# V's weight behind K's on one queue, a skip term seeded by VectorE, a scan over every sixteenth token, and a new step list, in a gated mix of a state-space layer and linear attention

## The chip, the cores and the metric

One core of one Trainium2 chip. The metric is device time in microseconds, median of the runs; lower is better. ACT is ScalarE, DVE is VectorE, PE is TensorE, POOL is GpSimd, SP is SyncE, which here only issues DMAs.

## The reference, cut to what matters

```python
x = A_x                                       # [1, 2048, 512], bf16
g = sigmoid((x * gate_w).sum(-1))             # one gate per token
# a: diagonal complex state space, 512 states
dt = exp(log_dt); Lam_bar = exp(dt * Lam)
Bu = x @ (((Lam_bar - 1) / Lam)[:, None] * Bmat).T
for t in range(2048):
    h = Lam_bar * h + Bu[t]                   # hseq[t] = h
a = 2 * (hseq @ Cmat.T).real + x * Dskip
# b: linear attention, 32 heads of 16, features softmax(+p) and softmax(-p)
q, k, v = split(x @ wqkv)
phi_q, phi_k = feat(q @ w_phi), feat(k @ w_phi)     # 32 features a head
b = ((phi_q @ (phi_k.T @ v)) / (phi_q @ phi_k.sum(0) + 1e-6)) @ wo
out = g * a + (1 - g) * b
```

## The kernel before

The 2048 tokens are 16 tiles of 128, ordered by residue: with NR = 8, tile pair r holds the tokens t with t mod 8 = r, 256 of each residue (NC = 256). `x_load` brings each tile transposed into `xT` by a DMA on SP's queue.

The whole kernel is one hand-written order. Each step is a generator (`st_k`, `st_g`, ...) that yields after each of its parts. The text `ORDER` names which step's next part is issued, the PSUM banks that it takes (`k3@6`), and the engine that empties PSUM where that isn't ACT (`:D` for DVE; `:A` puts an output DMA on ACT's queue). Instructions of PE, DVE, ACT and SP stand on each engine in that order; nothing is reordered. An instruction whose data or bank isn't ready stops its engine.

The steps, in about the order of their places in the list:

- W, f, w fold `w_phi` into K's and Q's weight. V, U, P, P2, P3, P4 and M make the decay constants, M on POOL; i makes Sin and Cos tables `T2s`, `T2c` on ACT over NC columns; D builds the diagonal blocks `dg`.
- k and v multiply `xT` with K's and V's weight; ACT copies the results out of PSUM into `Xq` and `vx`. v computes both 256-column halves of a tile in one step and takes two banks. V's weight `Wv` comes by one DMA on SP's queue between two groups of x tiles; K's comes on ACT's queue.
- x, n, e, s turn K into features, for five groups of tiles: maximum and minimum trees on DVE (x, n), Exp on ACT (e), sum trees on DVE, then Ln and Exp of the sums on ACT (s). a accumulates features times V. X, N, E, S do the same for Q.
- g (residue r, state block j) is B times x plus, for odd r, two earlier residues through `dg`: a recurrence unrolled over eight tokens. ACT copies it into `uv`, for r = 7 into `va`. z runs the scan over every eighth token on DVE, 256 columns: rotate by the tables, scan with r^8, rotate back, write into `H7`. h then gets the other residues' states from `H7`.
- q, c (scale C on ACT, add on DVE), y (states times C, then x times the diagonal `Dd` on PE for the skip term, into one PSUM bank), o (features times KV, Ln and Exp on ACT for the division, product on DVE, transpose), t (times `wo` onto the same bank, scaled by the gate into `ot`, DMA out).

Two steps set ACT's function tables. At the start, and in step L, `pin_act_set` issues a load of the set `natural_log_exp_and_others`; the Sin batch of i and P2, P3 comes between. Step L also ends the pool of the table steps and opens the pool of z. In the list of before it stands here:

```python
k6@7 R1 L e0 n1 n1 x1 n1 l13 k6:D v4@14 x1 ...
```

Of the kernel before, what the change touches and what calls it, by code (L numbers as in the profile page):

```python
# [10 lines left out]
ALU = mybir.AluOpType  # L11
# [9 lines left out]
P = 128  # L21
# [15 lines left out]
g63@0 z2 z2 v12@74 a3 nA v11 a3 xA g03 z2 z2 z2 z2 xA nA s4 J3 g63 g23@2 c5 s4 v12 g23 h51@6 g13@3 g13 g13 z2 z2 c0 z2
z2 eA g43@0 g43 eA v14@74 v14 J1 h51 s4 g33@2 g33 h52@3 g33 h12@0 g53@6 eA g53 g53 h12 h11@7 h11 h52 eA sA g73@4 g73
g73 g73 v13@26 v13 q10@0 z3 c6 z3 c5 sA z3 z3 v15@73 z3 a4 a4 a4 v15 z3 q10 q5@4 a4 Y z3 h31@0 q5 sA h30@4 z3 q9@2 h31
q13@6 h31 q9 h33@0 h61@7 Y q13 h30 sA sA c5 h62@3 z3 z3 h30 h61 sA Y Y h22@5 q4@2 h62 q4 h33 q15@6 q11@7 h22 h20@4 h20  # L40
h32@2 h32 sA sA c1 q11 h13@1 h13 h32 q14@3 h40@5 h33 c3 h53@7 h42@4 sA h42 h53 c1 c1 sA h21@2 c3 h21 q6@0 q6 q15 c6
q7@1 h63@4 h63 q8@7 h03@0 c3 q7 c6 h40 sA c7 h41@6 h41 y6@2 c7 h03 h03 h43@4 h43 y2@1 h02@5 c7 sA h23@6 h23 h01@0
h00@4 END q8 G X1 y6 y6 q14 y2 N1 X1 h00 h00 N1 y2 h02 h02 X1 N1 G h01 o0@6 y0@7 o0 o0@3 h01 o2@4 o2 X1 o2@5 o2 o2 N1
y5@6 o0 y3@0 X1 N1 y5 X2 o0 o1@4 E1 o2 y0 o2 o0 E1 E1 E1 X2 y1@5 y1 y3 y3 o1 G N2 X2 N2 X2 o0 N2 X2 o3@3 o3 o3@4 S1 o3
o3 G S1 N2 S1 t2 o3 S1 o3 t2 t2:A q12@3 q12 N2 S1 S1 o1@4 o1 o1 o1 o1 S1 S1 E2 S1 y0 y4@1 y9@3 y8@4 y8 y8 X3 E2 E2 S1
S1 S1 N3 X3 E2 t3 X3 X3 X3 S2 N3 t0 t0 t0:A S2 t3 S2 y1 t1 t1 y5 y9 y9 o4@7 o4 o4@0 o4 y4 o4 o4 o4 o5@5 o5 o5@7 o5 o5
y13@0 S2 S2 o6@5 o6 o6@7 o6 o6 y13 N3 y7@5 y7 N3 y7 y13 o5 S2 S2 N3 E3 o5 o6 o6 S2 S2 E3 E3 o7@7 o7:D y4 t4 t4:D t5
o7@7 S2 S2 E3 S3 t5 S2 S3 S3 o7 o7 o7 t6 y11@1 y11 o7 t6 o8@6 o8 o8@7 o8 o8 S3 S3 o8 y12@2 o9@6 o9 o9@7 o8 y11 y12 y12
y10@6 o9 o9 o9 o11@7 o11 o9 S3 S3 y10 y10 o11@7 t7 o11 o11 t7 t8 S3 S3 o11 o11 S3 t8 S3@7 S3:D S3@5 S3 t9 t9 t1:A
o10@4 y15@7 o10:D o10@5 o10:D t8 o10 o10 o10 y15 o12@4 o12:D o12@3 t4 o14@5 o12 o12 o12 t5 o14 t11 o14@4 o14:D o14 o14  # L50
t11 y14@3 t9:A o13@5 o13 o12@4 o12:D y14 o13@1 o13 o13 o15@4 o15:D o15@5 o15 o15 t12 t3:A t10 o13 o13@1 o15 t6:A t11
o14@4 o13:D t7 t10 t10 y15 t12 t12 o15@5 o15 y14 o14:D t13 t14 t14 t14 t13 t13 t15 t15 t15:A
"""
H_VECTOR = tuple((r, j) for r in (1, 2, 4, 5, 6) for j in range(4))
PH_PE = (14, 15)
H_SEED = tuple((r, j) for r in (0, 3,) for j in range(4))
# [14 lines left out]
def kernel(  # L71
# [27 lines left out]
    NC = S // NR  # L99
    NT2 = Pst // 64  # L100
# [7 lines left out]
    out_par = out2.rearrange("(a c r) d -> c r a d", r=NR, c=P)  # L108
# [59 lines left out]
    for k0 in (0, 2):  # L168
        nc.scalar.dma_start(out=wk_nat[:, k0:k0 + 2, :], in_=B_wqkv[k0 * P:(k0 + 2) * P, D:2 * D].rearrange("(k p) n -> p k n", p=P))
    nc.sync.dma_start(out=Wc[:], in_=B_w_phi.rearrange("(k hl) e f -> (hl e) k f", hl=8))  # L170
# [23 lines left out]
    H7 = pR.tile([P, NT2, ZP + NC], BF16, name="H7")  # L194
# [7 lines left out]
    dg = pBC.tile([P, 4, NT2, P], BF16, name="dg")  # L202
# [4 lines left out]
    par = pBC.tile([P, 22, PT], F32, name="ssm_par")  # L207
    dl = pBC.tile([P, 20, PT], F32, name="dl")
    dgB = pBC.tile([P, 10, PT, 2], F32, name="dgB")
    dgv = phT0[:, 3].rearrange("p m f -> p (m f)")[:, 0:32 * NT2].rearrange("p (k f) -> p k f", f=4)  # L210
# [10 lines left out]
    T2c = pAC.tile([P, PT, NC], BF16, name="T2c")  # L221
    T2s = pAC.tile([P, PT, NC], BF16, name="T2s")
    uv = [pAC.tile([P, 7, 2, NC], BF16, name=f"uv{j}") for j in range(PT)]
    va = [pAC.tile([P, 2, NC], BF16, name=f"va{j}") for j in range(PT)]
# [4 lines left out]
    x_res = x2.rearrange("(a c r) d -> r a c d", r=NR, c=P)  # L229
# [11 lines left out]
    nc.sync.dma_start(out=Wv, in_=B_wqkv[:, 2 * D:3 * D].rearrange("(k p) n -> p k n", p=P))  # L241
# [8 lines left out]
    iot = tabp.tile([P, NC], F32, name="iot", bufs=1)  # L250
    nc.gpsimd.iota(iot[:], pattern=[[1, NC]], base=0, channel_multiplier=0, allow_small_or_imprecise_dtypes=True)
# [15 lines left out]
    dt_, r_, om_, t0, t1, t2, den_, r2_, r4_, om8, r8_ = (par[:, 10 + k, :] for k in range(11))  # L267
# [102 lines left out]
    def st_P4():  # L370
        VS(out=om8, in0=t0, scalar1=float(NR), scalar2=None, op0=ALU.mult)
# [10 lines left out]
    def st_M():  # L382
# [24 lines left out]
        GT(out=dl[:, 9, :], in0=tb[:, 0, :], in1=den_, op=ALU.mult)  # L407
        GT(out=dl[:, 8, :], in0=tb[:, 1, :], in1=den_, op=ALU.mult)
        lo = dl[:, 0:10, :].rearrange("p (k t) j -> p k t j", t=2)
        up = dl[:, 10:20, :].rearrange("p (k t) j -> p k t j", t=2)  # L410
        GS(out=up[:, 0:4, 0], in0=lo[:, 0:4, 1], scalar1=-1.0, scalar2=None, op0=ALU.mult)
        GC(out=up[:, 0:4, 1], in_=lo[:, 0:4, 0])
        GS(out=up[:, 4, 0], in0=lo[:, 4, 0], scalar1=-1.0, scalar2=None, op0=ALU.mult)
        GC(out=up[:, 4, 1], in_=lo[:, 4, 1])
        for h in range(2):
            for ri in range(2):
                GC(out=dgB[ri * 64:(ri + 1) * 64, :, :, h], in_=dl[h * 64:(h + 1) * 64, 10 * ri:10 * ri + 10, :])
        yield

    def st_D():  # L420
        v5_ = dgv.rearrange("p (k t a) f -> p k t a f", k=4, a=2)
        b5_ = dgB[:, 0:8].rearrange("p (k a) j h -> p k a (j h)", a=2)
        for a in range(2):
            nc.vector.tensor_copy(out=v5_[:, :, :, a, :], in_=b5_[:, :, a, :].unsqueeze(3).to_broadcast([P, 4, NT2, 4]))
        VT(out=idn2[:], in0=ident[:, 0:64], in1=ident[:, 64:P], op=ALU.add)
        VT(out=dg[:].rearrange("p k t (a c f) -> p (k t a) c f", f=4, a=2),
           in0=idn2[:].rearrange("p (c f) -> p c f", f=4).unsqueeze(1).to_broadcast([P, 8 * NT2, 16, 4]),
           in1=dgv.unsqueeze(2).to_broadcast([P, 8 * NT2, 16, 4]), op=ALU.mult)
        yield
# [15 lines left out]
    def st_i(j):  # L445
        kk_ = tabp.tile([P, NC], F32, name="kk")
        VS(out=kk_[:], in0=iot[:], scalar1=om8[:, j:j + 1], scalar2=MAGIC, op0=ALU.mult, op1=ALU.add)
        yield
        psi = tabp.tile([P, NC], F32, name="psi")
# [37 lines left out]
    def st_v(ti):  # L487
        hd = D // 2
        pv = [bank([P, hd + c], F32, "pv") for c in range(2)]
        for kt in range(KT):  # L490
            for c in range(2):
                MM(out=pv[c][:], lhsT=xT[:, kt, ti * P:(ti + 1) * P], rhs=Wvg[:, kt, c * hd:(c + 1) * hd + c], start=(kt == 0), stop=(kt == KT - 1))  # L492
        yield
        for c in range(2):
            evac(vxb[ti % NVX][:, 16 * c:16 * c + 16, 0:Dh], pv[c][:, 0:hd].rearrange("p (h e) -> p h e", e=Dh))
# [369 lines left out]
```

## Time and profile before

| | |
|---|---|
| runs | 156.17, 156.59, 157.39 us; median 156.59 |
| profiled execution | span 153.7 us from first to last instruction; its time with what lies around the span is not listed |
| PE busy | 145.5 us, 95% of the span, 1238 matmuls |
| ACT busy | 136.7 us, 89% |
| DVE busy | 131.0 us, 85% |
| POOL busy | 12.9 us, 8% |
| granted TensorE clock | 0.995 |
| DMA | 17.03 MB, mean 111 GB/s |

Busy time is a share of the whole span. The kernel has stages with different limits, so busy time by stage and the chain of waits say more than these shares. In the rows of groups the time of one instruction is from its start to its end; instructions that follow each other on an engine overlap a little, so the chain's lengths, counted end to end, are shorter.

### The profile page before, as it was taken

The numbers are of one execution on the slowest core, as the hardware profiler recorded it, in microseconds if no ns is written. First come the engines' busy times: TensorE is split into PE (matmuls) and PEld (weight loads), VectorE is DVE, ScalarE is ACT, GpSimd is POOL, SyncE is SP. The second block draws the span as 40 slices with busy tenths as digits, with TensorE's granted clock in tenths as the row PEclk, the third lists the DMA queues.
The fourth block names the chain that finished last, engine by engine and source line by source line (L and its number), as shares of the span: only waits on it lengthen the run. The fifth ranks groups of instructions, "written<-read, shape, count | busy, mean of one in ns | idle before, by whom it ended". The sixth has DMA issues, their size and how long they took to land.

```text
span 153.7 us, 3412 instructions
## 1 busy us (share of the span) xinstructions
PE 145.5 (95%) x1238; PEld 99.7 (65%) x1254; DVE 131.0 (85%) x302; ACT 136.7 (89%) x322; POOL 12.9 (8%) x43
## 2 busy tenths in 40 slices
PE   7799999999999999999999999999999899999990
PEld 7656665886899858889876565554545455555550
DVE  3599999999999999999999999999999858445510
ACT  3599999999999999999999999999798897577672
POOL 8258800000000000000000000000000000000000
PEclk9999999999999999999999999999999999999998
DMA  4788995544474379960000006603139938667633
GB/s 117 162 220 121 213 171 102 102 86 92 101 102 100 80 146 205 237 133 0 2 4 2 0 0 134 125 18 68 33 82 118 215 80 194 141 118 172 211 123 102
DMA packets 48737, 17.03 MB, mean 111 GB/s; under 512 B 42064, under 2 KB 48720, under 8 KB 48720
## 3 DMA queue, kind: packets, MB, share of 16 engines
q1 hardware_dynamic: 47008, 15.36, 50.6%
q10 hardware_dynamic: 1552, 1.44, 2.9%
q8 instruction: 10, 0.16, 0.5%
q0 software_dynamic: 160, 0.01, 0.2%
q14 instruction: 7, 0.06, 0.1%
HBM read 2.64 MB, written 2.10 MB: 31 GB/s over the span
## 4 chain that ended last, share of the span: by engine, by line
ACT 48%; PE 31%; DMA 8%; DVE 6%; issue 3%; POOL 2%; ACTq 0%; POOLq 0%
PE py L734 12%; ACT EEk L140 12%; ACT uv L121 9%; PE py L782 6%; ACT vx L121 5%; PE pq L478 5%; ACT Xq L121 5%; ACT phT L603 4%; PE ph L685 3%; ACT va L121 3%; DMA phT<-EEq 3%; DMA oT<-on 3%; PE pn L753 2%; DMA vec_n<-in_A_log_dt_dram 2%; ACT EEq L140 2%
## 5 line engine op out<-in xcount | busy, mean ns | idle before, releaser
L614 PE MATMUL pgq<-xT,BT 128*128 128x256 bf16 x256 | 31.5, 272 | 0.0
L614 PEld LDWEIGHTS <-BT 128*128 128x128 bf16 x256 | 24.7, 98 | 3.5
L140 ACT ACTIVATE EEk<-EEk 128x1024 bf16<-128x1024 bf16 x20 | 21.3, 1099 | 0.0
L478 PEld LDWEIGHTS <-xT 128*128 128x128 bf16 x128 | 12.2, 97 | 11.0 <-issue 0.2
L121 ACT CAST uv<-pgq 128x512 bf16<-128x512 f32 x28 | 16.7, 638 | 0.0
L492 PE MATMUL pv<-Wv,xT 128*128 128x256 bf16 (+1 forms) x128 | 16.5, 273 | 0.1
L478 PE MATMUL pq<-Wq,xT 128*128 128x512 bf16 x60 | 15.2, 379 | 0.2
L782 PE MATMUL py<-Wo,oT 128*128 128x512 bf16 x59 | 14.7, 379 | 0.6 <-DMA oT<-on 0.3
L478 PE MATMUL pk<-Wk,xT 128*128 128x512 bf16 x60 | 14.9, 379 | 0.2
L492 PEld LDWEIGHTS <-xT 128*128 128x128 bf16 x128 | 12.5, 98 | 3.1 <-issue 0.2
L786 ACT ACTIVATE ot<-py,G 128x512 bf16<-128x512 f32 x15 | 9.8, 684 | 2.9 <-PE py L782 2.4
L140 ACT ACTIVATE EEq<-EEq 128x1024 bf16<-128x1024 bf16 x12 | 11.8, 1084 | 0.3 <-DVE EEq L535 0.3
L603 ACT ACTIVATE phT<-X,dgB 128x512 bf16<-128x512 bf16 x16 | 11.1, 751 | 0.0
L140 ACT ACTIVATE ld<-pn 128x16 f32<-128x16 f32 x32 | 6.4, 204 | 5.2 <-PE pn L753 5.0
L121 ACT CAST vx<-pv 128x256 bf16<-128x256 f32 x32 | 10.7, 435 | 0.0
L121 ACT CAST nu<-pn 128x256 bf16<-128x256 f32 x26 | 10.0, 400 | 0.0
L556 DVE TENSOR_TENSOR EEk<-EEk,rck 128x4096 bf16<-128x4096 bf16 (+1 forms) x5 | 9.3, 1860 | 0.1
L121 ACT CAST Xq<-pq 128x512 bf16<-128x512 f32 x16 | 9.0, 604 | 0.4 <-PE pn L753 0.4
L782 PEld LDWEIGHTS <-oT 128*128 128x128 bf16 x64 | 5.7, 98 | 5.7 <-DMA oT<-on 0.5
L753 PEld LDWEIGHTS <-phT 128*128 128x128 bf16 x128 | 6.4, 97 | 4.6 <-DMA phT<-EEq 1.3
L761 DVE TENSOR_TENSOR on<-nu,rd 128x512 bf16<-128x512 bf16 x16 | 6.6, 422 | 2.6 <-ACT rd L140 2.1
L519 DVE TENSOR_TENSOR smk<-smk 128x512 bf16<-128x512 bf16 (+4 forms) x18 | 8.1, 449 | 0.1
(179 smaller groups left out, 322.9 us busy)
## 6 DMA issues: line engine op xcount, KB each, us to landing
X<-HM SPq DMA_DIRECT2D x8, 256.0 KB, 4.7
out_dram<-ot SPq DMA_DIRECT2D x9, 128.0 KB, 2.2
out_dram<-ot ACTq DMA_DIRECT2D x7, 128.0 KB, 2.0
C2r<-in_B_wqkv_dram ACTq DMA_DIRECT2D x2, 256.0 KB, 3.5
Wv<-in_B_wqkv_dram SPq DMA_DIRECT2D x1, 512.0 KB, 4.0
Bn<-in_A_B_im_dram SPq DMA_DIRECT2D x1, 512.0 KB, 5.5
Bn<-in_A_B_re_dram SPq DMA_DIRECT2D x1, 512.0 KB, 5.9
Wo<-in_B_wo_dram SPq DMA_DIRECT2D x1, 512.0 KB, 5.9
```

What stands on the lines that cost most here:

```text
L121: nc.scalar.copy(out=out_ap, in_=in_ap)
L140: ins = nc.scalar.activation(**kw)
L478: MM(out=pt[:], lhsT=xT[:, kt, ti * P:(ti + 1) * P], rhs=W[:, kt, :], start=(kt == 0), stop=(kt == KT - 1))
L492: MM(out=pv[c][:], lhsT=xT[:, kt, ti * P:(ti + 1) * P], rhs=Wvg[:, kt, c * hd:(c + 1) * hd + c], start=(kt == 0), stop=(kt == KT - 1))
L519: VT(out=dst, in0=cur[:, :, :, 0:n, :], in1=cur[:, :, :, n:2 * n, :], op=op)
L556: VT(out=E5, in0=E5, in1=rc.to_broadcast([P, L, 2 * NB, Dh, 4]), op=ALU.mult)
L603: nc.scalar.mul(out=t_, in_=x_, mul=c_)
L614: MM(out=pg[:, h, :], lhsT=BT[:, kt, 2 * j + h, :], rhs=xT[:, kt, r * NC:(r + 1) * NC], start=(h == 0 and kt == 0), stop=(r % 2 == 0 and k ...
L734: MM(out=py[:], lhsT=hs(r, t, slice(a * P, (a + 1) * P)), rhs=C2B[t], start=(t == 0), stop=False)
L753: MM(out=pn[:, 4 * m:4 * m + 4, :].rearrange("p h e -> p (h e)"), lhsT=ph[:, 4 * hf + m, :], rhs=KVm[:, 4 * hf + m, :], start=(m == 0), st ...
L782: MM(out=py[:], lhsT=oT[:, g, :], rhs=Wo[:, g, :], start=False, stop=(g == HG - 1))
L786: nc.scalar.mul(out=ot[:], in_=py[:], mul=G[:, ti:ti + 1])
```

## The change

- V's weight comes in two DMAs on ACT's queue behind K's, no longer on SP's. The step v becomes two steps, u for the first 256 columns and v for the other 256 and the gate column, one bank each.
- Tokens within a residue are split by the parity of their place: the first tile of a pair holds tokens t with t mod 16 = r, the second those with t mod 16 = r + 8. The scan runs over N2 = 128 columns with r^16; g for r = 7 first forms the pair sums (`ua`, two matmuls with a new block `dg[4]`), and a new step Z gives the states of the places between.
- For the last eight tiles in order (`Y_SEED`), y starts with DVE's product x * Dskip written into the PSUM bank, and the matmuls of states and C accumulate onto it; the four `Dd` matmuls of such a tile go. A new step XN loads those x rows and Dskip on SP's queue.
- The list `ORDER` is new throughout. The F steps behind the first are gone. L stands here:

```python
s2 w0@0 x4 s2 g70 w1@3 g41 e3 e3 g62@2 x4 g11 a2 a2 g70 a2 a2 C0 s3 L g70 z0 s3 z0 ...
```

The core of the diff:

```diff
-    nc.sync.dma_start(out=Wv, in_=B_wqkv[:, 2 * D:3 * D].rearrange("(k p) n -> p k n", p=P))
+    for k0 in (0, 2):
+        nc.scalar.dma_start(out=Wv[:, k0:k0 + 2, :], in_=B_wqkv[k0 * P:(k0 + 2) * P, 2 * D:3 * D].rearrange("(k p) n -> p k n", p=P))
...
-    x_res = x2.rearrange("(a c r) d -> r a c d", r=NR, c=P)
+    x_res = x2.rearrange("(c a r) d -> r a c d", r=NR, c=P)
...
+        cmul(8, m4, m4)
...
+        GT(out=r16_, in0=r8_, in1=r8_, op=ALU.mult)
...
-    def st_v(ti):
+    def st_v(ti, c):
...
+        evac(ua[j][:], pg[:, :, 0:N2])
+        yield
+        for h in range(2):
+            MM(out=pg[:, h, N2:NC], lhsT=dg[:, 4, 2 * j + h, :], rhs=ua[j][:, h, :], start=False, stop=True, skip_group_check=True)
+        yield
         for h in range(2):
             for ri in range(2):
-                evac(va[j][h * 64:(h + 1) * 64, ri, :], pg[ri * 64:(ri + 1) * 64, h, :])
+                evac(va[j][h * 64:(h + 1) * 64, ri, :], pg[ri * 64:(ri + 1) * 64, h, N2:NC])
...
-        rb = r8_[:, j:j + 1].to_broadcast([P, NC])
+        rb = r16_[:, j:j + 1].to_broadcast([P, N2])
...
+    def st_Z(j):
+        pz = bank([P, 2, N2], F32, "pz")
+        for h in range(2):
+            MM(out=pz[:, h, :], lhsT=dg[:, 4, 2 * j + h, :], rhs=H7[:, 2 * j + h, ZP - 1:ZP - 1 + N2], start=(h == 0), stop=True, skip_group_check=True)
+        yield
+        VT(out=H7[:, 2 * j:2 * j + 2, ZP + N2:ZP + NC], in0=pz[:], in1=ua[j][:], op=ALU.add)
+        yield
...
+    def st_XN():
+        nc.sync.dma_start(out=live["Db"][:], in_=A_Dskip.unsqueeze(0).to_broadcast([P, D]))
+        yield
+        for h in range(4):
+            ti = order[8 + 2 * h]
+            for a in range(2):
+                assert order[8 + 2 * h + a] == ti + a
+            nc.sync.dma_start(out=live["xn"][:, 2 * h:2 * h + 2, :], in_=x2.rearrange("(c a r) d -> r c a d", r=NR, c=P)[ti // 2])
+            yield
...
+        if n in Y_SEED:
+            VT(out=py[:], in0=live["xn"][:, n - 8, :], in1=live["Db"][:], op=ALU.mult)
+            yield
         for t in range(NT2):
-            MM(out=py[:], lhsT=hs(r, t, slice(a * P, (a + 1) * P)), rhs=C2B[t], start=(t == 0), stop=False)
+            MM(out=py[:], lhsT=hs(r, t, slice(a * P, (a + 1) * P)), rhs=C2B[t], start=(t == 0 and n not in Y_SEED), stop=False, skip_group_check=n in Y_SEED)
             if t % 4 == 3:
                 yield
+        if n in Y_SEED:
+            return
```

More of the change, by code (lines that the diff above doesn't have):

```diff
@@ L55 @@
 PH_PE = (14, 15)
+Y_SEED = tuple(range(8, 16))
 H_SEED = tuple((r, j) for r in (0, 3,) for j in range(4))
@@ L220 @@
     BT = pAC.tile([P, KT, NT2, P], BF16, name="BT")
-    T2c = pAC.tile([P, PT, NC], BF16, name="T2c")
-    T2s = pAC.tile([P, PT, NC], BF16, name="T2s")
+    T2c = pAC.tile([P, PT, N2], BF16, name="T2c")
+    T2s = pAC.tile([P, PT, N2], BF16, name="T2s")
     uv = [pAC.tile([P, 7, 2, NC], BF16, name=f"uv{j}") for j in range(PT)]
-    va = [pAC.tile([P, 2, NC], BF16, name=f"va{j}") for j in range(PT)]
+    va = [pAC.tile([P, 2, N2], BF16, name=f"va{j}") for j in range(PT)]
+    ua = [pAC.tile([P, 2, N2], BF16, name=f"ua{j}") for j in range(PT)]
     X1 = pAC.tile([P, NT2, D], BF16, name="X1")
@@ L266 @@
     tb = par[:, 4:6, :]
-    dt_, r_, om_, t0, t1, t2, den_, r2_, r4_, om8, r8_ = (par[:, 10 + k, :] for k in range(11))
+    dt_, r_, om_, t0, t1, t2, den_, r2_, r4_, om8, r8_, r16_ = (par[:, 10 + k, :] for k in range(12))
     GT = nc.gpsimd.tensor_tensor
@@ L370, in st_P4 @@
     def st_P4():
-        VS(out=om8, in0=t0, scalar1=float(NR), scalar2=None, op0=ALU.mult)
+        VS(out=om8, in0=t0, scalar1=float(2 * NR), scalar2=None, op0=ALU.mult)
         yield
@@ L485, in st_k @@
         yield
-    def st_v(ti):
+    def st_v(ti, c):
         hd = D // 2
-        pv = [bank([P, hd + c], F32, "pv") for c in range(2)]
+        pv = bank([P, hd + c], F32, "pv")
         for kt in range(KT):
-            for c in range(2):
-                MM(out=pv[c][:], lhsT=xT[:, kt, ti * P:(ti + 1) * P], rhs=Wvg[:, kt, c * hd:(c + 1) * hd + c], start=(kt == 0), stop=(kt == KT - 1))
+            MM(out=pv[:], lhsT=xT[:, kt, ti * P:(ti + 1) * P], rhs=Wvg[:, kt, c * hd:(c + 1) * hd + c], start=(kt == 0), stop=(kt == KT - 1))
         yield
-        for c in range(2):
-            evac(vxb[ti % NVX][:, 16 * c:16 * c + 16, 0:Dh], pv[c][:, 0:hd].rearrange("p (h e) -> p h e", e=Dh))
-        nc.scalar.copy(out=gl[:, ti:ti + 1], in_=pv[1][:, hd:hd + 1])
+        evac(vxb[ti % NVX][:, 16 * c:16 * c + 16, 0:Dh], pv[:, 0:hd].rearrange("p (h e) -> p h e", e=Dh))
+        if c:
+            nc.scalar.copy(out=gl[:, ti:ti + 1], in_=pv[:, hd:hd + 1])
         yield
@@ L781, in st_t @@
         for g in range(HG):
-            MM(out=py[:], lhsT=oT[:, g, :], rhs=Wo[:, g, :], start=False, stop=(g == HG - 1))
+            MM(out=py[:], lhsT=oT[:, g, :], rhs=Wo[:, g, :], start=False, stop=(g == HG - 1), skip_group_check=n in Y_SEED)
         yield
@@ L831 @@
         next(st[tok])
-    for key in ("op", "fq", "eq", "sq"):
+    for key in ("xn", "op", "fq", "eq", "sq"):
         pools[key][0].__exit__(None, None, None)
```

142 lines of the change are left out of this document (75 added, 67 removed).

## The prediction

> **What bounds the kernel now.** I read the busy time by stage first: start and end in us, length, then PE, PEld, DVE, ACT and POOL busy with instruction counts, granted clock, DMA share and GB/s.
>
> ```profile
> 0.00:10.00 10.00, 7.81 (x73) 6.42 (x75) 5.66 (x37) 5.64 (x10) 4.92 (x17) 1.00 0.62 162
> 10.00:18.00 8.00, 7.95 (x52) 4.75 (x52) 7.93 (x29) 7.97 (x22) 7.34 (x24) 1.00 0.98 161
> 18.00:50.00 32.00, 31.87 (x310) 25.37 (x310) 31.69 (x63) 31.83 (x71) 0.66 (x3) 1.00 0.62 112
> 50.00:84.00 34.00, 33.68 (x325) 27.58 (x326) 33.67 (x69) 33.74 (x77) 0.00 (x0) 1.00 0.44 91
> 84.00:101.00 17.00, 16.70 (x105) 9.72 (x107) 16.71 (x41) 16.94 (x35) 0.00 (x0) 1.00 0.32 63
> 101.00:120.00 19.00, 18.53 (x138) 9.67 (x138) 18.64 (x36) 17.06 (x43) 0.00 (x0) 1.00 0.45 77
> 120.00:130.00 10.00, 9.91 (x80) 5.15 (x79) 7.85 (x16) 8.67 (x25) 0.00 (x0) 1.00 0.68 151
> 130.00:153.70 23.70, 19.11 (x171) 11.08 (x173) 8.86 (x20) 14.80 (x47) 0.00 (x0) 0.97 0.57 144
> ```
>
> From 18 to 101 us PE, DVE and ACT are all full; ACT has 0.49 us idle in 83. Nothing can be added to any of them there for free. After 101 us ACT and then DVE have room, and PE alone stays full.
>
> The chain that ended last says which of the three ends last (start, length, what, count). Its shares are in units of work that follow each other without a gap, so these lengths are also what one more such instruction costs a full engine.
>
> ```profile
> 19.94 0.54 ACT vx L121 x2
> 21.15 0.95 ACT EEk L140
> 29.39 0.97 ACT uv L121 x2
> 45.10 0.37 ACT va L121
> 62.68 1.83 ACT phT L603 x3
> 84.64 0.86 PE pq L478 x4
> 97.04 0.22 PE ph L685 x2
> 98.12 0.22 PE py L739 x4
> ```
>
> The chain runs on ACT from 18.9 to 84.2 us, then on PE. So ACT's list sets the first stage, PE's list the last one; from 84 to 101 us the chain names PE, but ACT is busy 16.94 of 17, so a longer ACT list lengthens that stretch as well. The hand-over that I use as a mark is the first Ln of the output steps (`ld<-pn`), which stands in ACT's timeline here, with the start of the Exp work:
>
> ```profile
> 0.79 1.07 ACTq L169 DMA_DIRECT2D C2r<-in_B_wqkv_dram  x2
> 5.39 1.07 ACT L121 COPY Xq<-ptw 128x512 bf16<-128x512 bf16 x2 [2.22 <-PE ptw L277]
> 16.93 0.64 ACT L121 CAST Xq<-pk 128x512 bf16<-128x512 f32 x1
> 17.59 1.28 ACT L132 ACT_TABLE_LOAD   x1
> 18.89 1.06 ACT L140 ACTIVATE EEk<-EEk 128x1024 bf16<-128x1024 bf16 x1
> 101.10 0.25 ACT L140 ACTIVATE ld<-pn 128x16 f32<-128x16 f32 x1
> ```
>
> **Part 1, the step list: seven more table loads on ACT.** Step L issues the pinned load of the table set that has both Exp and Ln. Before, L stands just ahead of the first e0. In the new list it stands behind all of e0 to e3, and behind s0 to s2, whose Ln and Exp alternate. Without the pinned set ahead of them the built program of the changed kernel places a load at each turn: ahead of the first EEk, then Ln, Exp, Ln, Exp, Ln, Exp of s0, s1 and s2, and L's own after them. That is 10 loads on ACT in all, where the program of before lists 3 and its trace shows these 3:
>
> ```profile
> L132 ACT ACT_TABLE_LOAD x2 | 2.6, 1283 | 1.9 <-issue 1.9
> L146 ACT ACT_TABLE_LOAD x1 | 1.3, 1283 | 0.0
> ```
>
> What a load costs is read from the timeline above: the copy ends at 16.93 + 0.64 = 17.57, the exponential behind the load at 18.89 + 1.06 = 19.95. That is 2.38 us, of which the exponential alone would take 0.95 back to back: 1.43 a load, because the load also breaks the overlap of its neighbours. 7 x 1.43 = +10.0 us. (Bounds: the bare 1.28 gives 9.0, less the 0.5 that ACT idles; the upper end is a rival below.) Behind each load wait the copies that empty PSUM for k, v and g tiles; PE waits for their banks, DVE for PE's tiles.
>
> The Trainium skill's page "ScalarE: Activation LUTs", section "What ACT_TABLE_LOAD costs", puts a switch at 1283 ns plus about 1380 ns of drain, 2.66 us. By that the seven would be 18.6 us, 8.6 more than my term. The trace agrees on the 1283 and shows no such drain: 0.02 us lie between 17.57 and 17.59.
>
> **The rest of ACT's list up to the first `ld`.** Four `ua` copies of 128x256 at 0.54/2 = +1.1. The scan over every sixteenth token halves the columns of `va` and of the Sin tables: two `vx` of 256 columns take 0.54 and two `uv` of 512 take 0.97, so 128 columns are 0.11. `va` goes from 16 x 0.37 to 14 x 0.26 = -2.3 (two move to DVE). Eight Sin at -0.11 = -0.9. One Wk, one Xq, one uv copy (0.49 each) and one phT scaling (1.83/3) go to DVE: -2.1. Two Wk copies of 0.49 stand behind the first `ld` now: -1.0. ACT's list to the first `ld`: 10.0 + 1.1 - 2.3 - 0.9 - 2.1 - 1.0 = **+4.8 us**.
>
> **PE behind that mark.** Behind its first `pn` PE has 8 more matmuls of 512 columns (0.86/4 each), 6 more of 256 (0.22/2), and 28 fewer of 128 (0.22/4): 1.7 + 0.7 - 1.5 = **+0.8 us**. The 32 `Dd` matmuls dropped for eight tiles are 1.8 us of PE in the whole, and 16 new ones of 128 columns (on `ua`, and Z) give 0.9 back; the list moves other work behind the mark.
>
> **DVE.** The skip term is eight 128x512 products into PSUM, which no row shows. The nearest are a 128x512 add out of PSUM and one within SBUF:
>
> ```profile
> L689 DVE TENSOR_TENSOR HM<-ph,uv 128x512 bf16<-128x512 f32 x8 | 5.3, 682 | 0.0
> L519 DVE TENSOR_TENSOR mxk<-mxk 128x512 bf16<-128x512 bf16 x4 | 1.7, 418 | 0.0
> L654 DVE TENSOR_TENSOR_SCAN w<-ssm_par,ut 128x256 bf16<-128x256 f32 x8 | 5.1, 675 | 0.0
> ```
>
> I take the PSUM row, 0.6 to 0.68, 5 us in all; by the SBUF row 3.3. Five of them stand behind 120 us, where DVE idles 2.15 of 10 and then 14.8 of 23.7 us: nothing. Three stand ahead of the second group's rho product, where DVE is full: 0 to 2.0, and they delay that group's phT transposes and the matmuls on them. I take **+0.6**, one of three, since the idle time just behind takes the others. What is saved in the scan steps (at most half of 5.1 us of scans; four new adds from PSUM at 0.68 take 2.7 back), in the tables, and the larger D are worth nothing either way while ACT's list ends last; were ACT not late, each DVE us would count, as DVE idles 0.6 us in these 66.
>
> **Start and queues.**
>
> ```profile
> 6.58 0.58 SPq L241 DMA_DIRECT2D Wv<-in_B_wqkv_dram  x1
> 61.75 2.23 SPq L304 DMA_DIRECT2D X<-HM  x3
> SPq L775 <- DVE mxq L519: 5.8, 1, 5.8
> L829 PE MATMUL spin<-fillw 128*128 128x128 bf16 x36 | 3.9, 292 | 1.1 <-DVE fillw L159 1.1
> ```
>
> V's weight behind K's adds two issues, 1.07 us, ahead of ACT's first table load; ACT then idles 2.22 us for PE anyway, so 0. If its bytes delay K's, whose landing PE awaits, up to +1. SP loses 0.58 us of issue ahead of x tiles 4 to 7, so their k steps can start up to 0.6 earlier, and V's halves fill PE there. Eight fill matmuls go (8 x 0.055). ACT idles 4.4 us of its first 10; I take **-0.4** (bounds -1.0 and +1.0).
> SP gets five more issues, Db and four of xn, at 2.23/3 = 0.74 each, among the oT transposes. SP waits 5.8 us for DVE there at one place alone, so nothing; without that cover the oT transposes behind them are up to 3.7 us later, and the last projections with them. POOL's longer M stands on an engine with 0.66 us of work from 18 to 50: nothing, and late it would hold D on DVE. x tiles and output rows keep 1 KB rows at another stride: nothing.
>
> **The sum.** 4.8 + 0.8 + 0.6 - 0.4 = +5.8 us on the profiled span of 153.7, 159.5. The median of the runs shown is 156.59, 2.9 us over the span (start and end around it, taken as unchanged): 162.4 us.
>
> **Rivals.**
> (a) As summed, the loads paid in full: 162.4; its own range 159.5 to 165.5, from loads at 9.0 less idle time, seeds at 0 and the early start, up to all three seeds, a late K weight and ACT's lateness passed on to DVE and back. For it: ACT's 0.49 us idle in 83. Chance 0.62.
> (b) Not slower: the loads go unpaid. Place: ACT from 18 to 50 us. A load waits for no data, so it can run while the Ln or Exp behind it waits for DVE's sum; in the new list ACT has 5.2 us less of other work in the stage, so it may wait there. Price: the 10.0 falls away, -5.2 + 0.8 + 0.6 - 0.4 = -4.2, 152.4 us. It decides once ACT would wait some 6 us beside the loads before 84 us. Against it: PE and DVE have no more than 0.7 us to give, so they would make ACT wait only if they themselves are slower. Chance 0.10.
> (c) Half of it: loads hidden in part, PE's list ends last, with 0.9 fewer matmul us, -0.4 at the start and +0.6 for the seeds: 155.9, no difference. Chance 0.10.
> (d) The tail gives way too: all three seeds and SP's five issues on the path, 162.4 + 1.4 + 3.7 = 167.5. For it: DMA 0.68 busy from 120 to 130 us, PE with 0.1 idle. Against: SP's waits. Chance 0.14.
> (e) A load lets ACT run empty first, for as long as a whole 1.06 us exponential: 7 x 1.06 = 7.4 more, 169.8. Against: 0.02 us in this trace. Chance 0.04. (That is the skill's drain, named above, at a price from rows.)
>
> **How the numbers follow.** Likeliest: 162.4. The range 156.0 to 168.0 takes in (a), (d) and the upper half of (c) and leaves out (b), (e) and the other half, 0.19. A difference under 1%, 1.6 us, can hardly be told from none here: faster 0.10 from (b), same 0.10 from (c), slower 0.80 from (a), (d), (e).
>
> **What would show it.** Right: ten ACT_TABLE_LOADs, eight between 15 and 55 us, each 1.28 long and with no gap before it; ACT still full from 18 us; the first `ld` at 105 to 107 us instead of 101.1; PE with 4 to 6 us more of idle between 18 and 60, ended by ACT's copies; from the first `ld` to the end 53 to 55 us (52.6 before). Seeds near 0.65. Wrong: the first `ld` at 100 us or earlier although the loads are there (then ACT's list did not bind), fewer than ten loads, or a lengthening that lies behind the first `ld`.

## The result, and the profile after

| | before | after |
|---|---|---|
| runs | 156.17 to 157.39 us, median 156.5 (4) | 165.32 to 165.65 us, median 165.46 (4) |
| profiled execution | span 153.7 us | span 163.3 us, time 165.32 us |
| start of the first Exp of the features | 18.89 us | 18.79 us |
| first `ld` (the prediction's mark) | 101.10 us | 107.65 us |
| from the mark to the end | 52.6 us | 55.65 us |

The changed kernel is slower: ratio 1.0574, 95% interval 1.054 to 1.0608. The forecast was 162.4 us with a range of 156.0 to 168.0. Between the first Exp and the mark 6.65 us are lost, behind the mark 3.05. Two of the kernels further down had one slow run each, at a lower granted clock, which is left out of their figures.

The busy time by stage, after, with the same columns as in the prediction:

```profile
18.00:50.00 32.00, 28.63 (x235) 21.51 (x236) 25.67 (x50) 31.72 (x61) 5.16 (x16) 0.95 0.62 115
50.00:84.00 34.00, 30.50 (x314) 25.35 (x313) 31.05 (x75) 33.61 (x73) 0.00 (x0) 1.00 0.35 71
84.00:101.00 17.00, 16.89 (x149) 12.21 (x150) 16.86 (x40) 16.88 (x39) 0.00 (x0) 1.00 0.07 14
101.00:120.00 19.00, 18.82 (x136) 10.47 (x137) 18.71 (x41) 17.79 (x44) 0.00 (x0) 1.00 0.71 131
120.00:130.00 10.00, 9.64 (x71) 4.88 (x71) 9.29 (x19) 8.44 (x23) 0.00 (x0) 1.00 0.85 167
```

From 18 to 84 us ACT is as full as before (65.33 of 66 us). PE has fallen from 65.55 to 59.13 us and DVE from 65.36 to 56.73: both now wait for ACT, which has no more to give. What fills ACT are the loads, here in its timeline (start, length, operation):

```profile
17.50 1.28 ACT L144 ACT_TABLE_LOAD   x1
18.79 1.06 ACT L144 ACTIVATE EEk<-EEk 128x1024 bf16<-128x1024 bf16 x1
...
26.93 1.28 ACT L144 ACT_TABLE_LOAD   x1
29.02 1.28 ACT L144 ACT_TABLE_LOAD   x1
33.53 1.28 ACT L144 ACT_TABLE_LOAD   x1
36.11 1.28 ACT L144 ACT_TABLE_LOAD   x1
...
47.77 1.28 ACT L144 ACT_TABLE_LOAD   x1
49.76 1.28 ACT L144 ACT_TABLE_LOAD   x1
54.27 1.28 ACT L136 ACT_TABLE_LOAD   x1
```

The groups after have them as one row, seven loads with 0.1 us of idle ahead of all of them:

```profile
L144 ACT ACT_TABLE_LOAD x7 | 9.0, 1283 | 0.1
```

With L's own and two at the start there are ten. They come in pairs: Ln, then back to Exp, for the sums of s0, s1 and s2. The waits of PE and DVE up to the mark name the same place (engine, line and what it waited for, us in total, times, longest):

```profile
DVE EEk L563 <- ACT rck L144: 6.2, 3, 2.9
PE pv L499 <- ACT vx L125: 2.4, 1, 2.4
PE pgq L621 <- ACT uv L125: 1.7, 1, 1.7
PE pgq L621 <- ACT va L125: 1.1, 1, 1.1
```

`rck` is the Exp behind the second load of a pair. DVE waits three times, 2.9 us at the longest, before it can scale the features; PE waits for the copies that stand behind the loads.

### The profile page after: what moved, and what is told of

Its sections match the earlier page's. It is cut to its first block, busy times and chain, and to the rows that moved or that the text cites. A ratio compares the mean times of both kernels' runs of the same rounds, so it can differ in the third digit from the quotient of the medians.

```text
span 163.3 us, 3396 instructions
## 1 busy us (share of the span) xinstructions
PE 147.0 (90%) x1215; PEld 98.8 (61%) x1230; DVE 137.0 (84%) x326; ACT 139.8 (86%) x321; POOL 14.9 (9%) x47
## 4 chain that ended last, share of the span: by engine, by line
PE 38%; ACT 37%; DMA 11%; DVE 7%; issue 3%; SPq 1%
PE pgq L621 9%; ACT EEk L144 7%; PE pq L486 6%; PE pv L499 6%; ACT Xq L125 5%; DMA phT<-EEq 5%; ACT L144 5%; PE py L772 4%; ACT uv L125 3%; DMA xT<-in_A_x_dram 3%; DMA oT<-on 3%; PE py L822 3%; PE ph L707 3%; ACT vx L125 2%; PE kvacc L601 2%
## 5 line engine op out<-in xcount | busy, mean ns | idle before, releaser
L621 PE MATMUL pgq<-xT,BT 128*128 128x256 bf16 x256 | 32.2, 276 | 2.8 <-ACT uv L125 1.7
L499 PE MATMUL pv<-Wv,xT 128*128 128x257 bf16 (+1 forms) x128 | 18.4, 279 | 2.6 <-ACT vx L125 2.4
L822 PE MATMUL py<-Wo,oT 128*128 128x512 bf16 x62 | 15.3, 379 | 1.6 <-DMA oT<-on 1.5
L125 ACT CAST uv<-pgq 128x512 bf16<-128x512 f32 x27 | 15.7, 611 | 0.2
L125 ACT CAST vx<-pv 128x256 bf16<-128x256 f32 x32 | 12.1, 422 | 0.3 <-PE pv L499 0.3
L826 ACT ACTIVATE ot<-py,G 128x512 bf16<-128x512 f32 x11 | 7.5, 684 | 4.6 <-PE py L822 2.4
L610 ACT ACTIVATE phT<-X,dgB 128x512 bf16<-128x512 bf16 x15 | 11.1, 754 | 0.0
L793 PE MATMUL pn<-KVm,phT 128*128 128x68 bf16 x128 | 7.7, 194 | 1.1 <-DMA phT<-EEq 1.1
```

Of the source, the lines that this page charges most:

```text
L125: nc.scalar.copy(out=out_ap, in_=in_ap)
L499: MM(out=pv[:], lhsT=xT[:, kt, ti * P:(ti + 1) * P], rhs=Wvg[:, kt, c * hd:(c + 1) * hd + c], start=(kt == 0), stop=(kt == KT - 1))
L610: nc.scalar.mul(out=t_, in_=x_, mul=c_)
L621: MM(out=pg[:, h, :], lhsT=BT[:, kt, 2 * j + h, :], rhs=xT[:, kt, r * NC:(r + 1) * NC], start=(h == 0 and kt == 0), stop=(r % 2 == 0 and k ...
L793: MM(out=pn[:, 4 * m:4 * m + 4, :].rearrange("p h e -> p (h e)"), lhsT=ph[:, 4 * hf + m, :], rhs=KVm[:, 4 * hf + m, :], start=(m == 0), st ...
L822: MM(out=py[:], lhsT=oT[:, g, :], rhs=Wo[:, g, :], start=False, stop=(g == HG - 1), skip_group_check=n in Y_SEED)
```

## The experiments

The theory after the result: the seven extra loads cost about 1.3 to 1.6 us each, and the rest of the change nearly cancels. The rivals: the rest of the new list is what costs; the seeds or V's place cost. Each run's ratio is to the kernel before on the same chip in the same session (its medians lay between 156.28 and 156.77 us). Where two of the new kernels are compared below, the difference is that of their distances from the kernel before of their own session.

### The changed kernel with step L put early

```
-... i1 e0 ...  C0 s3 L g70 ...
+... i1 L e0 ...  C0 s3 g70 ...
```

> The changed kernel with step L alone moved, to just ahead of the first e0; three table loads instead of ten. Theory (loads paid in full on ACT's list): the 10.0 us of loads go, but ACT's other work in the stage is 5.2 us lighter than before, so PE and DVE become the end of it and not all comes back: 157 to 159.5 us, first ld at 100 to 102 us. Rival (what counts lies behind the first ld, in seeds, SP's queue and the transposes): 163 us or more, since that part is untouched. Rival (loads ran in ACT's own waits): 164 to 165.5.

Measured: 156.58 us, ratio 1.0018 [0.9993, 1.0044]; span 154.5. The move of one token in the list takes back 8.7 us. The mark is at 98.63 us, 9.02 earlier than in the changed kernel. Counted from the first Exp (at 18.58 us here) it is 80.05 us away instead of 88.86, which is 1.26 for each of the seven loads, no more than their length. Both time and mark lie somewhat below what was expected. All three engines are full again:

```profile
18.00:50.00 32.00, 31.69 (x308) 24.97 (x309) 31.70 (x64) 31.54 (x70) 4.96 (x15) 1.00 0.66 117
50.00:84.00 34.00, 33.90 (x334) 28.00 (x333) 33.33 (x78) 33.39 (x78) 0.00 (x0) 1.00 0.36 73
```

So the loads are the whole loss. All else together is worth 2.5 us up to the mark and costs 3.3 behind it (55.87 against 52.6), which nearly cancels.

### The kernel before with step L put late

```
-... R1 L e0 ...  C4 g70 g70 ...
+... R1 e0 ...  C4 L g70 g70 ...
```

> The kernel before with step L alone moved, to just ahead of the first z0, behind e0 to e3 and s0 to s2; ten table loads instead of three. Theory: each of the seven costs 1.3 to 1.43 us on a full ACT, 165.5 to 166.5 us, and the first ld near 111. Rival (loads run while ACT waits for DVE's sums): under 160.

Measured: 167.33 us, ratio 1.0709 [1.0673, 1.0745]. The mark moves from 101.10 to 112.19 us, 1.58 a load, and the tail stays (53.0). That is more than expected. Here the waits are longer than in the changed kernel, and they reach PE through DVE:

```profile
DVE EEk L556 <- ACT rck L140: 8.8, 3, 3.8
PE kvacc L594 <- DVE EEk L556: 5.2, 3, 2.3
```

ACT from the first Exp to the mark, before and then here (its busy time is the fourth after the length):

```profile
18.89:101.10 82.21, 81.45 (x729) 61.90 (x734) 81.28 (x167) 81.73 (x180) 0.00 (x0) 1.00 0.48 92
18.89:112.19 93.30, 85.00 (x728) 63.23 (x733) 81.62 (x168) 91.86 (x188) 0.00 (x0) 0.96 0.42 81
```

ACT is busy for 10.1 us more: 9.0 are the loads themselves, and the other 1.1 must be neighbours that no longer overlap, since the rest of ACT's list is the same. The remaining 1.0 is ACT waiting for engines that it had held up (1.44 us idle instead of 0.48). In the new list ACT is busy for 9.1 us more with the loads than with L early (88.05 against 78.92) and does not wait longer. So the old list suffers more from late loads than the new one, 11.1 against 9.0 us. PE's granted clock was also lower here (0.96 in this stretch, 0.98 in the changed kernel); whether that had a part, these runs don't settle.

### One extra load alone

Beside L early: a new step K pins the joint set at the early place, and L goes back to its late one. That makes one load more, which ran at 46.26 us.

```
+    def st_K():
+        pin_act_set()
+        yield
-... i1 L e0 ...  C0 s3 g70 ...
+... i1 K e0 ...  C0 s3 L g70 ...
```

> The kernel with the pinned set of Exp and Ln loaded ahead of the first e0 by a step of its own, and step L left where the change put it: four table loads in place of the three of the kernel with L moved, one extra at about 54 us, and all Ln and Exp between them served by one set. Theory A (each load is paid in full by ACT's list, at 1.3 to 1.6 us): 157.9 to 158.2 against 156.6, first ld at 99.9 to 100.2 instead of 98.6. Rival (a lone load hides, and only the run of seven in close order made the stall): 156.6 and first ld at 98.6.

Measured: 157.19 us, ratio 1.0032 [1.0006, 1.0057], mark at 99.64. Beside L early that is +0.3 in the runs, with intervals that overlap. In the profiled executions the way from the first Exp to the mark is 0.8 us longer (80.81 against 80.05), but in the kernel with one `xn` load below, which has no load more and the same list up to there, it is 0.6 longer too (80.68). So a lone load costs less than theory A said; that it costs anything is not shown.

### V's weight, alone and taken away

The first kernel is the one before with only V's two issues on ACT's queue:

```
+    for k0 in (0, 2):
+        nc.scalar.dma_start(out=Wv[:, k0:k0 + 2, :], in_=B_wqkv[k0 * P:(k0 + 2) * P, 2 * D:3 * D]...)
-    nc.sync.dma_start(out=Wv, in_=B_wqkv[:, 2 * D:3 * D]...)
```

> The kernel before with V's weight in two DMAs behind K's on ACT's queue instead of on SP's, list unchanged. In the changed kernel's trace ACT's first table load starts at 4.49 us instead of 1.89 and ACT is busy 4.36 us of the first 10 instead of 5.64. Theory (the two issues hold ACT and K's weight arrives later): 157.3 to 158, +0.8 to +1.5. Rival (hidden behind ACT's wait for PE, as forecast): 155.9 to 156.6.

Measured: 157.96 us, ratio 1.011 [1.0071, 1.0149], 1.7 us slower. PE's list has the transposes of the small vectors ahead of much of the start's work, and those vectors come late. The DMA issue (KB, us to landing), then the transpose in PE's timeline, with its wait in brackets:

```profile
vec_n<-in_A_Lambda_im_dram POOLq DMA_DIRECT2D x1, 1.0 KB, 6.2
```

```profile
8.80 0.16 PE L314 MATMUL pvt<-ident,vec_n 12*128 12x12 bf16 x1 [2.11 <-DMA vec_n<-in_A_log_dt_dram]
```

In the kernel before, the same transfer landed in 4.2 us and the transpose began at 6.78. From 10 to 18 us ACT and DVE have lost 1.22 and 0.79 us, and PE's granted clock is 0.79 (it was 1.00):

```profile
10.00:18.00 8.00, 7.78 (x43) 4.26 (x44) 7.14 (x31) 6.75 (x16) 5.92 (x22) 0.79 0.95 132
```

The first Exp starts at 22.25 us instead of 18.89, and from there to the mark the two kernels take the same 82.2 us. But the loss is not the same in every run, and goes with the clock: the two of the ten runs with a granted clock of 0.995 took 156.83 us, the eight with 0.978 to 0.989 took 157.64 to 159.02. The two are only 0.5 us above the kernel before. So most of the loss goes with the low clock behind PE's wait; whether that wait was shorter in those two runs isn't recorded.

Then the opposite, L early with V's weight back on SP's queue:

```
-    for k0 in (0, 2):
-        nc.scalar.dma_start(out=Wv[:, k0:k0 + 2, :], ...)
+    nc.sync.dma_start(out=Wv, in_=B_wqkv[:, 2 * D:3 * D]...)
```

> The kernel with step L ahead of the first e0, and V's weight back on SP's queue in one issue among the x tiles, as before the change. Theory A (V's two issues on ACT's queue make the small loads and the pvt transpose late, which costs 1.7 us where they are added to the kernel before alone): the vec_n loads land near 4.2 us again, the pvt transpose starts near 6.8 instead of 7.25, the first ld falls from 98.6 to about 98.1 and the time from 156.6 to about 156.1. Theory B (the place of V's weight was paid for in the new list, whose v steps on half a weight start earlier): V lands later than the first u step wants it, PE waits there, and the time is 157 or more. The wait of PE for Wv, and the time of the pvt transpose, tell them apart.

Measured: 160.02 us, ratio 1.021 [1.018, 1.0239]; 3.1 us slower than L early. That is theory B, which had 157 or more. The waits up to 18 us:

```profile
DVE vec L327 <- PE pvt L325: 4.5, 1, 4.5
PE pv L498 <- DMA Wv<-in_B_wqkv_dram: 2.9, 1, 2.9
```

The small vectors do land sooner (3.0 to 3.5 us after their issue), but the new list has the first half of V ahead of the second small transpose on PE. PE waits for `Wv`, and the transpose stands behind it, at 14.09 us instead of 9.77. The granted clock was 0.985 to 0.989 in all six runs, and 0.996 to 1.000 in those of L early, so a part of the 3.1 us may again be the clock. The third, L early with V's two issues behind ACT's first table load:

```
+    pin_act_set()
     for k0 in (0, 2):
         nc.scalar.dma_start(out=Wv[:, k0:k0 + 2, :], ...)
-    pin_act_set()
```

> The kernel with step L ahead of the first e0, and V's two DMAs still on ACT's queue, but issued behind ACT's first pinned table load instead of ahead of it. Theory A (what V's issues cost is the crowding of the first microseconds: the table load starts 2.6 us later and the small loads land later): table load at 1.9 us again, pvt near 6.8, time about 156.0. Theory B (nothing at the start reaches the end here, since PE has list work enough): 156.6, no difference. If ACT's issues then stand in the way of its first Xq copies, pk starts later and the time is over 157.

Measured: 158.53 us, ratio 1.0112 [1.0068, 1.0155]. Theories A and B missed, and the last case of the three came: the load did start at 1.90 us, but V's issues then held ACT's first copies into `Xq` for 3.7 us. V came later as well, PE waited 1.7 us for it, and the second small transpose stood behind (DVE waited 3.2 us).

```profile
ACT Xq L125 <- DMA Wv<-in_B_wqkv_dram: 3.7, 1, 3.7
```

V's place and the list belong together: the queue that costs 1.7 us in the old list is worth 3.1 in the new one.

### The seeds

L early, with the skip term of all tiles on PE and no loads of `Db` and `xn`:

```
-Y_SEED = tuple(range(8, 16))
+Y_SEED = ()
```

> The changed kernel with L ahead of e0 and the skip term of all tiles on PE again (no seeds, no XN loads; the list otherwise as it is). Against the run with L alone moved. Theory: DVE wins 3 seeds (2 us) where it is full, PE loses 1.8 us: -1.0 to +1.0. Rival (seeds and xn loads make the tail 2 us longer than forecast): -2 to -3.

Measured: 159.72 us, ratio 1.0217 [1.018, 1.0254]. The seeds are worth 3.1 us, with the cost of their loads taken off. What they take from PE shows in the stretch from the mark to the end (L early with its seeds first, then without):

```profile
98.63:154.50 55.87, 48.67 (x362) 25.19 (x366) 43.74 (x87) 38.53 (x108) 0.00 (x0) 1.00 0.69 138
```

```profile
99.08:157.90 58.82, 51.06 (x393) 27.61 (x398) 39.33 (x79) 38.71 (x108) 0.00 (x0) 1.00 0.52 111
```

PE has 2.39 us less, DVE 4.41 us more, and the stretch is 2.95 shorter: there DVE has room and PE has none. But the DMA share rises from 0.52 to 0.69. So next L early with one of the four xn loads:

```
-            nc.sync.dma_start(out=live["xn"][:, 2 * h:2 * h + 2, :], ...)
+            if h == 0:
+                nc.sync.dma_start(out=live["xn"][:, 0:2, :], ...)
-            VT(out=py[:], in0=live["xn"][:, n - 8, :], in1=live["Db"][:], op=ALU.mult)
+            VT(out=py[:], in0=live["xn"][:, n % 2, :], in1=live["Db"][:], op=ALU.mult)
```

> The kernel with step L ahead of the first e0, and of the four xn loads only the first is issued; the skip term of all eight tiles is then made from that one pair, so the output is not the reference's in six tiles. Instructions of DVE and PE are the same. Theory A (the xn loads, 2 KB rows of 128 partitions among the phT transposes of SP's queue, are why phT lands in 3.8 us instead of 2.8, and with it the tail of 55.9 us instead of 52.6): phT lands in 3.1 or less and the time falls by 0.5 to 1.0, to about 155.8. Rival (the phT transposes are late for the list's own order, or for the oT transposes that stand with them): 156.6, within 0.3.

Measured: 155.17 us, ratio 0.9897 [0.9865, 0.9928]. Beside L early 1.7 us for three loads of 256 KB, more than expected; the stretch from the mark to the end is 54.06 us instead of 55.87. The phT transposes (the last number is the median us to landing) in L early, and PE's waits for them there (0.8 and 0.3 us with one load):

```profile
phT<-EEq SPq DMA_TRANSPOSE x10, 3.8
```

```profile
PEld L793 <- DMA phT<-EEq: 4.4, 4, 1.4
PE pn L793 <- DMA phT<-EEq: 2.8, 4, 0.9
```

The same transposes with one load:

```profile
phT<-EEq SPq DMA_TRANSPOSE x10, 3.0
```

The time from a transpose's issue to its landing is what changed, so the transfers are slower while the xn rows move beside them. This kernel leaves out issues and bytes together; if it is the bytes, they should cost less at another time. All five issues ahead of the first oT transpose:

```
-X2 XN o2 ... y5@6 XN o0 ... y5 XN N2 ... o1 o3 XN o1 ... S2 XN S2
+X2 XN XN XN XN XN o2 ... y5@6 o0 ... y5 N2 ... o1 o3 o1 ... S2 S2
```

> The kernel with step L ahead of the first e0, and the five issues for Db and xn one after the other where the first of them stood, at about 98 to 103 us, ahead of the first oT transpose, instead of spread up to 123 us. Theory A (what the xn loads cost is their bytes beside the phT and oT transposes behind 104 us, since with one pair loaded the tail was 54.1 us instead of 55.9): phT lands in about 3.0 us instead of 3.8 and the time falls by 1.0 to 1.4, to 155.2 to 155.6, which would beat the kernel before (156.6). Rival (the same bytes cost the same wherever they go, now by holding up the first oT transposes): 156.6, within 0.3.

Measured: 155.76 us, ratio 0.9954 [0.993, 0.9978], the one version of the whole computation here that beats the kernel before, by half a per cent; 0.9 is gained of the 1.7. phT lands in 3.4 us and PE's wait for it falls (1.4 us in total, 0.8 at the longest).

The same five issues, at the places of the changed list but on POOL's queue:

```
-            nc.sync.dma_start(out=live["xn"]...)
+            nc.gpsimd.dma_start(out=live["xn"]...)
```

> The kernel with step L ahead of the first e0, and the five issues for Db and xn at their old places in the list but on POOL's queue, where nothing else is issued and POOL is idle. Theory A (the bytes on the 16 DMA engines are what slows the transposes): no gain over 156.6, or a loss if POOL's queue issues slower; as POOL has nothing ahead of the loads they can also start earlier than on SP's queue, and then up to 1.4 are gained. Rival (the order within SP's queue is what costs: a transpose waits behind an xn load in the same queue): phT lands in about 3.0 us and the time is about 155.3, with the loads still spread beside the transposes. Where the loads start tells the two apart.

Measured: 163.64 us, ratio 1.0458 [1.0417, 1.0498], 7.0 us lost. POOL has nothing ahead of them and issues all from 89.3 us on, as soon as their buffer is free, beside the first phT transposes and the load of Wo. POOL's timeline, the DMA issues, and PE's wait:

```profile
90.27 2.85 POOL L754 DMA_DIRECT2D xn<-in_A_x_dram  x4 [0.32 <-DVE EEk L574]
```

```profile
Wo<-in_B_wo_dram SPq DMA_DIRECT2D x1, 512.0 KB, 11.1
...
phT<-EEk SPq DMA_TRANSPOSE x4, 9.5
```

```profile
PE pn L793 <- DMA phT<-EEk: 5.8, 1, 5.8
```

With the loads on SP's queue phT<-EEk landed in 3.9 us and Wo in 4.3. The run moved the loads in time as well as to another queue, so its 7.0 us are not the price of the queue; but loads on POOL's queue did slow transposes on SP's. Another queue is no other path. The Trainium skill says the same on "DMA: Bandwidth & Descriptors", section "Issuing engines are not separate DMA queues": what any engine issues runs on the same 16 DMA engines, interleaved. The trace agrees, with 9.5 us for 3.9.

Last, half of the seeds, with the loads that they need:

```
-Y_SEED = tuple(range(8, 16))
+Y_SEED = tuple(range(12, 16))
```

> The kernel with step L ahead of the first e0, only the last four of the tiles seeded by DVE (the other four have their skip term as matmuls on PE, as before), and Db and two xn loads one after the other at about 98 us. Theory A (a seed saves PE's four 128-column matmuls and its wait in the tail, eight are worth 3.1 us, half of them half): 1.5 lost beside the kernel with the five issues together, so about 156.9. Rival (DVE, at 13.6 of 28 us in the last stage, and the loads eat up a part of what the first four seeds bring): at or below the time with eight seeds.

Measured: 157.79 us, ratio 1.0097 [1.0066, 1.0128], 2.0 over eight seeds with the issues together, more than the 1.5 expected. Between no seeds and that kernel lie 4.0 us, so the first four seeds are worth about as much as the last four.

### The scan

L early, with the scan over every eighth token again:

```
-    N2 = NC // 2
+    N2 = NC
-            rb = r16_[:, j:j + 1]...   # and no ua copies, no step Z, dg of 4 blocks
+            rb = r8_[:, j:j + 1]...
```

> The kernel with step L ahead of the first e0 and with the scan over every eighth token again, as before the change (va, the Sin tables and the scan 256 columns wide, no ua copies, no step Z); list, V in halves and seeds as in the changed kernel. Theory A (the narrower scan shortens ACT's list, which ends last up to the first ld: here 14 va copies at 0.37 instead of 0.26 and eight Sin at 0.11 more, less four ua copies of 0.27): +1.4, first ld near 100.0 and time near 158.0. Rival B (the scan's form is worth nothing: what ACT loses DVE, PE or the waits take back, since step Z and its adds on DVE out of PSUM are gone): 156.6, within 0.5. Rival C (the wider scans on DVE, at 0.68 against about half of it, bind in 84 to 99 us, where DVE is full): 159 or more, with PE and ACT waiting there.

Measured: 162.62 us, ratio 1.0366 [1.0307, 1.0426], 5.5 us slower than L early; mark at 103.68. Rival C, and earlier than it said, from 50 us on. The stage, and the scans here and with L early alone:

```profile
50.00:84.00 34.00, 31.44 (x287) 25.57 (x286) 33.51 (x70) 31.59 (x66) 0.00 (x0) 1.00 0.35 74
```

```profile
L660 DVE TENSOR_TENSOR_SCAN w<-ssm_par,ut 128x256 bf16<-128x256 f32 x8 | 5.1, 680 | 0.0
```

```profile
L666 DVE TENSOR_TENSOR_SCAN w<-ssm_par,ut 128x128 bf16<-128x128 f32 x8 | 2.9, 405 | 0.0
```

DVE is the full engine there, and PE and ACT wait 2.5 and 1.8 us more than with L early alone. Of the 5.2 us that the profiled span grows, 3.6 lie between the first Exp and the mark; 1.4 lie ahead of it, where the Exp starts at 20.02 us instead of 18.58, in part behind Sin tables that are twice as wide. The new list is written for the narrow scan and the old one carries the wide scan with a mark at 101.1, so the 5.5 us are the narrow scan's worth in this list, not in any list.

## Why the prediction was right in its direction and 3 us short

**Step list and loads: right.** Ten loads, eight of them between 17.5 and 54.3 us, 1.283 long each. ACT stayed full and nothing hid them, so case (a) held; (b) and (c), with the loads unpaid in whole or in part, fell with L early: 8.7 us. The term was 10.0, the measured one 9.0 to 9.1: the bare length, almost without the broken overlap that 1.43 held. That overlap is real in the old list (10.1 us), so the price of a load depends on what stands beside it. The drain of about 1380 ns that the Trainium skill's page "ScalarE: Activation LUTs" states, section "What ACT_TABLE_LOAD costs", and with it case (e), didn't show: 0.1 us of idle stand ahead of seven loads.

**The rest of ACT's list: -5.2, measured -4.1, and the sum is luck.** ACT's busy and idle time up to the mark tell list and waits apart. Before, after, and with L early:

```profile
0.00:101.10 101.10, 98.10 (x857) 73.84 (x867) 95.75 (x234) 96.22 (x211) 12.92 (x43) 1.00 0.54 105
0.00:107.65 107.65, 98.39 (x855) 73.49 (x864) 93.21 (x240) 101.16 (x214) 14.88 (x47) 0.98 0.50 98
0.00:98.63 98.63, 96.00 (x855) 72.49 (x864) 92.69 (x240) 92.09 (x208) 14.88 (x47) 1.00 0.57 107
```

ACT is busy for 4.94 us more than before, where +4.8 was forecast. The loads were 1 us cheaper and the rest saved 1.1 less (96.22 to 92.09), so two misses cancel. No one term makes the 1.1. V in halves isn't it: with L early a `vx` copy that stands alone takes 0.27 us up to the next start, as each of a pair did before (0.54 for two).

```profile
15.18 0.42 ACT L125 CAST vx<-pv 128x256 bf16<-128x256 f32 x1
15.45 0.22 ACT L503 COPY gl<-pv 128x1 f32<-128x1 f32 x1
```

**The start: -0.4 forecast, +1.3 measured; this step failed.** The same rows give ACT's idle time up to the mark: 4.88 us before, 6.49 after. Of these 1.6 us more, 1.3 lie ahead of the first Exp, where ACT is idle for 4.40 us before and 5.67 after:

```profile
0.00:18.89 18.89, 16.64 (x131) 11.95 (x134) 14.48 (x68) 14.49 (x32) 12.92 (x43) 1.00 0.80 166
0.00:18.79 18.79, 16.51 (x123) 10.90 (x126) 13.73 (x68) 13.12 (x32) 10.51 (x36) 1.00 0.85 167
```

The prediction took K's 1.07 us for V's two issues and hid them behind ACT's wait of 2.22 us. They took 2.57, ACT's first load started 2.60 us later (4.49 for 1.89), and behind it ACT still waited 0.83 us for DVE's `vec`, where it had waited 0.23. The measured 1.3 lies outside the bounds of -1.0 and +1.0. The first Exp starts almost where it did, 0.1 earlier, only because ACT has 1.4 us less work ahead of it: narrower Sin tables, and copies that went to DVE, both counted in the -5.2 of the list. So the mark is 2.15 us later than forecast (107.65 against 105.5), 2.0 of it by ACT's idle time. No run takes V's issues away without making the list wait for V, so their price in the changed kernel is read from its trace and not shown by an experiment.

**PE behind the mark: +0.8, measured +1.13** (47.45 to 48.58).

**The seeds: too small a gain.** Their length was nearly right (0.695 us each, forecast 0.65), and so was DVE's room in the last stage. The prediction had +0.6 for DVE and, inside PE's +0.8, -1.8 for the 32 `Dd` matmuls: a net gain of 1.2. With L early the stretch behind the mark is 2.95 us shorter with the seeds than without, loads included, and PE is busy for 2.39 less there. That three seeds hold up the second group's product, no run shows by itself.

**SP's issues: nothing, measured +1.7 or more.** The prediction asked only when SP would be free to issue. It left out that the bytes move beside the transposes that PE waits for. Its own row had a DMA share of 0.68 from 120 to 130 us; after, it is 0.85. Case (d) is half true: the tail did give way, but by transfers that land late, where (d) had seeds and issues on the path. Of the 3.05 us behind the mark 1.1 are PE's work; the three xn loads cost 1.8 us there with L early (55.87 to 54.06). If the two add up in the changed kernel, 0.1 is left.

**The narrow scan on DVE: nothing while ACT's list ends last.** No run has the wide scan in the changed list with L late, so this isn't shown. With ACT relieved the scan is worth 5.5 us in this list, which fits the prediction's condition ("were ACT not late, each DVE us would count").

**The sum.** Mark 2.15 us later than forecast, tail 1.65 longer (55.65 against 54.0), and 2.0 us instead of 2.9 around the span: 2.9 in all, which leads from 162.4 to the profiled execution's 165.3. The signs named in advance were a mark at 105 to 107 us and a tail of 53 to 55; both were missed by 0.65. The 2.9 around the span was no step of the kernel: it set the span of one execution against the median of others.

## What to carry to other kernels

When a list is rewritten by hand or by a search, look first at where the function tables are pinned: on an engine with no idle time seven switches were paid at least by their length, and one token was worth 8.7 us here, more than all the rest of the change. Moving work to an engine with room pays by what it takes from the full one, but count the bytes it brings, and put them where no transfer on the path is moving. Whether an engine's saving is worth anything depends on which engine binds after the rest of the change, so price it on both sides of that point. And to check a term for one engine's list, take that engine's busy and idle time up to the mark: an early start that looks unchanged can be a longer wait and less work.

## What was not expected of the hardware

The granted TensorE clock fell to one half behind waits of little more than 2 us. After PE waited 2.38 us for a `vx` copy, the changed kernel shows:

```profile
31.43 0.81 PE L499 MATMUL pv<-Wv,xT 128*128 128x257 bf16 x4 [2.38 <-ACT vx L125]
```

The granted clock is the third number from the end of each row:

```profile
32.00:33.00 1.00, 1.00 (x19) 1.00 (x18) 1.00 (x6) 1.00 (x4) 0.00 (x0) 0.50 0.60 115
...
34.00:35.00 1.00, 1.00 (x6) 0.75 (x5) 1.00 (x2) 0.99 (x2) 0.00 (x0) 0.50 0.65 120
35.00:36.00 1.00, 0.95 (x7) 0.56 (x7) 1.00 (x2) 0.90 (x3) 0.00 (x0) 0.95 0.08 14
```

From the mean clock of 0.84 in the microsecond before and 0.95 behind, the half clock lasts about 0.3 + 3 + 0.1 = 3.4 us. The same size stands behind the wait of 2.11 us in the kernel with V's issues alone: 0.79 over 8 us is 3.4 us at half. The length of the wait alone doesn't decide: a wait of 1.69 us ended by `uv` in the changed kernel had full clock behind it, and one of 1.69 us for `Wv`, in the kernel with V's issues behind the load, half clock. The Trainium skill's page "TensorE: Matmul & The Clock Gate", section "What's actually happening", has the half rate behind an idle window of about 3.4 us that runs free of the kernel. Half rate and 3.4 us agree; but PE was busy for 1.02 of the 3.41 us ahead of the half clock, so less than a whole idle window suffices here, and the measurement decides.

```profile
28.26:31.67 3.41, 1.02 (x11) 0.77 (x9) 1.11 (x2) 3.38 (x7) 0.00 (x0) 1.00 0.40 91
```

What it costs is not the same everywhere. In the changed kernel ACT was full at the time, and the runs at a granted clock of 0.988 and 0.990 (165.41 and 165.32 us) were no slower than those at 0.999 and 1.000 (165.65 and 165.51). In the kernel with V's issues alone it fell into the start, and the runs with the lower clock were 0.8 to 2.2 us longer; what of that is the clock and what a longer wait ahead of it, they don't tell.

The other surprise is the issue on ACT's queue: K's two DMAs took 1.07 us there, V's two right behind them 2.60 (1.89 to 4.49 us with L early), and ACT's first load stood behind them. (The profile puts that wait down to the DMA of `Wc`; with V's issues behind the load, it started at 1.90 us.)

```profile
0.79 1.07 ACTq L173 DMA_DIRECT2D C2r<-in_B_wqkv_dram  x2
1.89 2.60 ACTq L175 DMA_DIRECT2D Wv<-in_B_wqkv_dram  x2
4.53 1.28 ACT L136 ACT_TABLE_LOAD   x1 [4.53 <-DMA Wc<-in_B_w_phi_dram]
```
